# Bucketed attention and a rational FFN on one core: the maxima of every pair one slot sooner, their transposition behind the values' first group

## The chip, the cores and the metric

One core of one Trainium2 chip runs the whole program in one launch. The metric is the device time of one execution in microseconds (us), as the median of several runs. The host only rearranges the inputs (q and k transposed per pair of heads, v by blocks of 128 rows) and puts a few small constants together.

## The reference, cut to what matters

```python
q_bits = (einsum('bhsd,dk->bhsk', q, proj) > 0)        # 6 bits a row
k_bits = (einsum('bhsd,dk->bhsk', k, proj) > 0)
mask   = bucket(q_bits)[..., :, None] == bucket(k_bits)[..., None, :]
scores = where(mask, (q @ k.T) / sqrt(64), -1e9)
scores = scores - scores.max(-1)
attn   = exp(scores);  attn = attn / (attn.sum(-1) + 1e-9)
x      = (attn @ v) as (tokens, heads * 64)            # 3072 x 512
h      = x @ w_in                                      # 3072 x 2048
g      = (a0 + a1 h + a2 h^2 + a3 h^3) / (1 + |b0||h| + |b1| h^2 + 1e-6)
out    = g @ w_out
```

There are 4 batches of 8 heads, 768 rows each, head dimension 64.

## The kernel before, in words

The 32 heads are worked in 16 *pairs* (p = 0 to 15), two heads at a time on the 128 partitions. q and k are split into a high part in a short float format and a low part (`high` on ScalarE, `low` on VectorE), and both parts are moved by DMAs into the operands Q1, K1 (high) and Q2, K2 (high and low crossed), so that two products together give exact scores.

The mask is folded into the product. `bits` multiplies q and k of two pairs with the projection (TensorE tile psb) and VectorE compares with zero (tile mb); this is done once for two pairs, in frames of even p. `penalties` scales one half of mb by 2 to the 60th on ScalarE, and `maskrows` moves the rows into rows 64 to 75 of Q1 and 64 to 76 of K1, with four DMAs. A product over 76 rows then has a huge negative term wherever a bit differs.

The row maximum has to be known before the scores are exponentiated. `maxstep` computes, for one of the twelve (head, block of 128 query rows), the 768 products of the high parts (two matmuls, tile psm) and VectorE reduces them to one column of M[p] (tile m). When the twelve columns are there, `shift_turn` transposes M[p] on TensorE (one matmul with the identity, tile pst, in PSUM tag "s"; for pair 15 in tag "psa"), VectorE copies it with the sign turned (tile mt), and `shift_rows` moves it by a DMA into row 76 of Q1. From then on the scores come out with the maximum already taken off.

`scores` does one of twelve steps (half of the query rows, block of 128 keys): for either head two matmuls (tile pss, tag "s", three PSUM buffers) and one exponential on ScalarE (tile E, f32). GpSimd adds the E of neighbouring steps (tile acc). `values` multiplies E with v (tile psv): six steps' values stand together as one group of 24 matmuls, once behind step 5 and once behind step 11. `values_out` copies the result (col, xo), `sums` adds up acc with a column of ones (psu), and DMAs store x and the sums to DRAM. Meanwhile `weights` loads blocks of w_in and w_out (64-bit floats), turns them into f32 and splits each into a high and a low part, on ScalarE and VectorE (tiles wr, ws, wi_hi, wi_lo, wo_d). After pair 15 the FFN runs (`Ffn.rest`, tiles psh and pso); nothing in it is touched.

The order of all this is written out by hand. `plan` (lines 474 to 481) is a list of places: `at(p, s, f, ...)` puts the call f at place 12 p + s, and the calls are issued in the order of their places. I call the places 12 f to 12 f + 11 *frame* f: in it the scores of pair f stand at whole places 0 to 11. Every engine, and SyncE with its DMA queue, works in this order. The places are in the tables `MID` (lines 41 to 48, the pairs in the middle), `FIRST` and `LAST` (the exceptions). Preparation runs ahead: for pair p the high and low parts, bits, penalties, mask rows and the first maxima stand in frame p - 2, the rest of the maxima, the transposition and its DMA in frame p - 1.

Two kinds of buffers matter for the order. PSUM tag "psa" has two buffers; each maxstep takes one, and so does psb. So a maxstep's product waits until the reduction two maxsteps before has ended. PSUM tag "s" has three buffers; each head of a scores step takes one, and so do psu and pst. So a head's products wait until the tile three takes before has been read.

The lines that are touched are 42 to 46 (the places of maxima, low, penalties, maskrows, shift_turn and of four steps of weights), 59 (two places for pairs 2 and 3) and 491 and 516 (which place a maxstep and a transposition take).

Of the kernel before, what the change touches and what calls it, by code (L numbers as in the profile page):

```python
# [38 lines left out]
ACCS = 5  # L39

MID = dict(
    group=6, values=[0.66, 0.05], values_out=3.5, maxima=7.17,
    maxima_steps=[0, 1.15, 1.73, 2.64, 3.32, 5.08, 5.86, 6.98, 8.0, 8.84, 10.26, 11.37], sums=14.65, sums_store=17.37,
    high=[-0.41, 1.19], low=[1.06, 3.35], bits=2.81, penalties=4.05, high_move=1.9, maskrows=5.61, second_low=-2.2,
    second_high=2.69, load_v=10.99, shift_turn=8.61, shift_rows=8.82, load=9.0, recips=[20.0, 22.0, 23.0],
    weights=[[1.44, 4.0, 4.1, 5.09, 5.49, 7.11, 9.5, 9.75, 17.5], [8.05, 10, 10.65, 11.5, 12.38, 14.29, 16.34, 19.32, 21.22]],
    weights_last=[0.5, 0.8, 1.0, 1.2],
)

# [2 lines left out]
    high_move=4.53, maskrows=8.2, second_low=4.25, second_high=4.35, load_v=4.78, group=2,  # L52
    values=[2.35, 2.65, 2.32, 2.35, 0.35, 0.61], values_out=3.02, high1=[-0.27, -5.58], low1=[11.24, 4.95],
    high_move1=20.05, load2=21.89, load3=3.8, penalties1=-6.57, maskrows1=3.69,
    weights=[[-5.7, 6.64, 6.7, 11.42, 12.19, 18.75, 21.75, 38.77, 44.13], [8.03, 9.04, 9.24, 11.12, 14.81, 15.27, 15.99, 17.91, 46.81]],
    warm=6, warms=[3, 3, 3, 1, 1, 1], maxima00=[-4.26, -2.29, -4.17, 1.67, -1.15, 2.77], shift00=[2.15, 4.99],
    shift0=[3.67, 3.44], ahead=3, scores=[[3.68, 3.82, 7.26], [6.03, 8.25, 12.4]], pen01=[4.77, 14.55], comp01=3.35,
    second_high0=[-2.86, 2.12, -3.42, 3.45], load_v0=20.9, bits1=5.23, comp1=[15.82, 11.68],
    maxima0=[3.11, -1.97, -0.5, 2.14, 2.86, 3.25], turn1=[8.46, 13.26], rows1=[9.59, 14.35],
)  # L60

LAST = dict(
    group=6, values=[0.28, 0.44], values_out=1.39, vout14=3.03,
    tokens=[[-15.0, -11.5, -8.6, -7.4], [-7.43, -5.11, -2.83, -1.09], [1.1, 4.2, 5.45, 6.3]], terms=1.0, ffn=[13.61, 16.09, 16.14],
    sums=16.96, wide=8, share=11, third=0, sums14=14.69, weights14=1.44, sumst14=22.46,
# [38 lines left out]
def bucket_attention_then_rational_ffn(ctx, tc, qT, kT, v, proj, w_in, w_out, coef, consts, out):  # L104
# [56 lines left out]
    def operands_to_terms():  # L161
# [3 lines left out]

    tail.tile([P, 32], F32, tag="below", name="below")
    last = attention(tc, nc, raw, ps_b, tail, tokens, early, operands_to_terms, ffn, load, QF, KF, v, w_in, w_out, wo_d, ident, cst,
                     ones, prj, wi_hi, wi_lo, x_d, s_d, r_d, coefficients)
    ffn.rest(ctx, last)
# [3 lines left out]
def attention(ctx, tc, nc, raw, ps_b, tail, tokens, early, operands_to_terms, ffn, load, QF, KF, v, w_in, w_out, wo_d, ident, cst, ones, prj,  # L173
# [243 lines left out]
    def recips(bb):  # L417
        n = 2 * NHP * S // P
        s = tail.tile([P, n], F32, tag="rs", name=f"rs{bb}")
        nc.sync.dma_start(s, s_d[bb].rearrange("h (x c) -> (h x) c", c=n))  # L420
        yield
        z = tail.tile([P, n], F32, tag="rz", name=f"rz{bb}")
        nc.vector.tensor_scalar(out=z, in0=s, scalar1=0.0, scalar2=S * TINY, op0=ALU.is_equal, op1=ALU.mult)
        nc.vector.tensor_tensor(out=z, in0=s, in1=z, op=ALU.add)
        nc.vector.tensor_scalar(out=s, in0=s, scalar1=0.0, scalar2=1e-9, op0=ALU.is_gt, op1=ALU.mult)
        nc.vector.tensor_tensor(out=z, in0=z, in1=s, op=ALU.add)
        nc.vector.reciprocal(out=s, in_=z)
        yield
        nc.sync.dma_start(r_d[bb].rearrange("h (x c) -> (h x) c", c=n), s)
        yield  # L430
# [45 lines left out]
    def at(p, s, f, *args):  # L476
        plan.setdefault(12 * p + s, []).append((f, args))

    def spread(p, steps, gen):
        for s in steps:  # L480
            at(p, s, lambda g: next(g, None), gen)

    for p in range(NPAIR):
        mid = 0 < p < NPAIR - 1
        n = MID["group"] if mid else (FIRST if p == 0 else LAST)["group"]
        for s in range(12):
            if p > 0 or s >= FIRST["ahead"]:
                at(p, s, scores, p, s)

            if p > 1:  # L490
                at(p - 2, MID["maxima"] + MID["maxima_steps"][s] if p > 2 else FIRST["maxima2"] + FIRST["rate2"] * s, maxstep, p, s)
            if s % n == n - 1:
                for i in range(s - n + 1, s + 1):
                    at(p, s + (MID["values"][s // n] if mid else (FIRST if p == 0 else LAST)["values"][s // n]), values, p, i)
            if s % NT == NT - 1:
                at(p, s + (LAST["vout14"] if (p, s) == (NPAIR - 2, 11) else MID["values_out"] if mid else (FIRST if p == 0 else LAST)["values_out"]), values_out, p, s // NT)
        for hf in range(2):
            at(p, 6 * hf + 9, values_store, p, hf)
        if p < NPAIR - 1:
            at(p, MID["sums"] if p < NPAIR - 2 else LAST["sums14"], sums, p)  # L500
            at(p, MID["sums_store"] if p < NPAIR - 2 else LAST["sumst14"], sums_store, p)
        if p > 1:
            for t in range(2):
                at(p - 2, (MID if p > 2 else FIRST)["high"][t], high, p, t)
                at(p - 2, (MID if p > 2 else FIRST)["low"][t], low, p, t, nc.vector if p > 2 else nc.gpsimd)
            if p % 2 == 0:
                at(p - 2, (MID if p > 2 else FIRST)["bits"], bits, p)
                at(p - 2, (MID if p > 2 else FIRST)["penalties"], penalties, p)
            at(p - 2, (MID if p > 2 else FIRST)["high_move"], high_move, p)
            at(p - 2, (MID if p > 2 else FIRST)["maskrows"], maskrows, p)  # L510
        if p > 0:
            at(p - 1, (MID if p > 1 else FIRST)["second_low"], second_low, p)
            at(p - 1, (MID if p > 1 else FIRST)["second_high"], second_high, p)
            at(p - 1, (MID if p > 1 else FIRST)["load_v"], load_v, p)
        if p > 1:
            at(p - 1, MID["shift_turn"], shift_turn, p)
            at(p - 1, MID["shift_rows"], shift_rows, p)
        if p > 3:
            at(p - 4, MID["load"], load, p)
        if p % NHP == NHP - 1 and p + 1 < NPAIR:  # L520
            spread(p, MID["recips"], recips(p // NHP))
# [308 lines left out]
```

## Time and profile before

| | |
|---|---|
| median of 3 runs | 930.67 us (930.5 to 931.36) |
| the profiled execution | 929.79 us |
| its span, first to last instruction | 928.0 us |
| TensorE (PE) busy | 920.8 us, 99% |
| weight loads (PEld) | 699.9 us, 75% |
| VectorE (DVE) | 842.0 us, 91% |
| ScalarE (ACT) | 647.6 us, 70% |
| GpSimd (POOL) | 435.8 us, 47% |
| granted TensorE clock | 1.000 |

A line of the timeline gives the start and the length in us, the engine, the line of the kernel, the operation, the tiles written and read, the shapes, how many instructions are merged, and in brackets the engine's idle time before it with what ended that. Since every instruction is issued through a helper, all have the line L93; the tiles tell them apart. The length of a merged matmul row reaches to the modelled end of its last matmul, which overlaps with the next row's start: how long TensorE took is best read from one start to the next. PEld is the loading of weights, DVEq, SPq and the like are the engines' instruction queues. A line of `waits` says which engine and tile waited for which, for how many us in total, how often, and for how long at most.

### The profile page before, as it was taken

What the parts mean: (1) busy time and instruction counts of PE and PEld (TensorE: products, weight loads), DVE (VectorE), ACT (ScalarE), POOL (GpSimd) and SP (SyncE); (2) the same over time, 40 slices, a digit from 0 to 9 for tenths busy, and PEclk for the clock granted to TensorE, in tenths of its full rate; (3) what the DMA queues carried; (4) which work ended last, traced back from release to release, by engine and by line L of the source; (5) the groups of instructions that cost most, each with busy time, mean ns of one, the idle gap of its engine ahead of it and who ended that gap; (6) DMA issues with size and microseconds to landing.
All of it is one profiled execution on the core that took longest, in us unless ns stands there. A gap on an engine that the chain in (4) does not pass through costs nothing.

```text
span 928.0 us, 13694 instructions
## 1 busy us (share of the span) xinstructions
PE 920.8 (99%) x4678; PEld 699.9 (75%) x4678; DVE 842.0 (91%) x1029; ACT 647.6 (70%) x1229; POOL 435.8 (47%) x361
## 2 busy tenths in 40 slices
PE   8999999999999999999999999999999999999998
PEld 4666766666767676668888888888888888888886
DVE  6799889888988898888998999899999999998996
ACT  6567767676767766887767766776676677667664
POOL 5587878787788877622222232223222322232221
PEclk9999999999999999999999999999999999999999
DMA  6767878878877777545402100400040003001001
GB/s 197 214 181 219 229 230 230 223 214 212 242 212 225 229 195 233 163 155 197 163 1 81 56 1 1 136 2 0 1 137 1 1 34 102 1 1 46 1 1 46
DMA packets 51098, 111.57 MB, mean 120 GB/s; under 512 B 9330, under 2 KB 19942, under 8 KB 51028
## 3 DMA queue, kind: packets, MB, share of 16 engines
q1 hardware_dynamic: 50596, 110.34, 40.5%
q8 instruction: 37, 0.61, 0.3%
q10 hardware_dynamic: 432, 0.36, 0.1%
q14 instruction: 33, 0.27, 0.1%
HBM read 56.82 MB, written 21.17 MB: 84 GB/s over the span
## 4 chain that ended last, share of the span: by engine, by line
PE 93%; DVE 4%; DMA 1%; SPq 0%; ACT 0%; issue 0%; DVEq 0%; ACTq 0%
PE psh L93 28%; PE pso L93 28%; PE pss L93 14%; PE psv L93 12%; PE psm L93 7%; PE psu L93 2%; DVE m L93 2%; DMA wr<-w_in 1%; PE psb L93 1%; DVE ws L93 1%; DVE wr L93 0%; SPq L93 0%; PE psw L93 0%; PE pst L93 0%; ACT E L93 0%
## 5 line engine op out<-in xcount | busy, mean ns | idle before, releaser
L93 POOL TENSOR_TENSOR gl<-c,gh 128x512 fp32r<-128x512 f32 x95 | 133.2, 1402 | 387.0 <-ACT gh L93 371.0
L93 ACT ACTIVATE E<-pss 128x384 f32<-128x384 f32 x384 | 167.5, 493 | 105.8 <-PE pss L93 91.9
L93 PE MATMUL pso<-wo,gh 128*128 128x512 f32 x768 | 236.2, 390 | 0.0
L93 DVE TENSOR_REDUCE m<-psm 128x1 f32<-128x768 f32 x192 | 179.5, 948 | 31.4 <-PE psm L93 28.2
L93 POOL TENSOR_TENSOR acc<-E,E 128x384 f32<-128x384 f32 x124 | 155.6, 1273 | 85.9 <-ACT E L93 85.7
L93 PE MATMUL pss<-q,k 128*128 128x384 f32 (+2 forms) x768 | 171.3, 347 | 0.3 <-ACT E L93 0.3
L93 PEld LDWEIGHTS pso<-wo,gh 128*128 128x128 f32 x768 | 144.3, 188 | 29.9
L93 PEld LDWEIGHTS pss<-q,k 128*128 128x128 f32 (+2 forms) x768 | 134.6, 190 | 29.1 <-issue 17.0
L93 PE MATMUL psh<-xh,wi_hi 128*128 128x512 f32 x384 | 149.8, 390 | 0.0
L93 PE MATMUL psh<-xl,wi_hi 128*128 128x512 f32 x384 | 149.7, 390 | 0.0
L93 PE MATMUL psh<-xh,wi_lo 128*128 128x512 f32 x384 | 149.6, 390 | 0.0
L93 PE MATMUL pso<-wo,gl 128*128 128x512 f32 x384 | 149.1, 390 | 0.0
L93 ACT ACTIVATE h<-psh 128x512 f32<-128x512 f32 x96 | 57.4, 598 | 130.5 <-PE psh L93 130.3
L93 POOL TENSOR_TENSOR acc<-acc,E 128x384 f32<-128x384 f32 x123 | 136.6, 1129 | 5.9 <-ACT E L93 5.7
L93 DVE SCALAR_TENSOR_TENSOR c<-c,ab,r 128x512 f32<-128x512 f32 x96 | 135.6, 1413 | 0.0
L93 PE MATMUL psv<-E,v 128*64 128x385 f32 x768 | 131.9, 492 | 0.0
L93 PE MATMUL psm<-k,q 76*128 76x384 f32 (+1 forms) x384 | 102.4, 349 | 1.6 <-DVE m L93 1.0
L93 PEld LDWEIGHTS psv<-E,v 128*64 128x64 f32 x768 | 52.2, 137 | 65.3 <-issue 63.7
L93 DVE SCALAR_TENSOR_TENSOR w<-h,absb,w 128x512 f32<-128x512 f32 x96 | 74.0, 771 | 16.2 <-ACT w L93 15.9
L93 PEld LDWEIGHTS psh<-xh,wi_hi 128*128 128x128 f32 x384 | 72.1, 188 | 16.1 <-issue 1.2
L93 PEld LDWEIGHTS psh<-xh,wi_lo 128*128 128x128 f32 x384 | 72.2, 188 | 14.9
L93 PEld LDWEIGHTS psh<-xl,wi_hi 128*128 128x128 f32 x384 | 72.1, 188 | 14.9
(78 smaller groups left out, 1221.3 us busy)
## 6 DMA issues: line engine op xcount, KB each, us to landing
q<-q SPq DMA_DIRECT2D x45, 192.0 KB
k<-k SPq DMA_DIRECT2D x45, 192.0 KB
wr<-w_in SPq DMA_DIRECT2D x16, 512.0 KB
wr<-w_out SPq DMA_DIRECT2D x16, 512.0 KB
wo_d<-wr SPq DMA_DIRECT2D x16, 512.0 KB
wo<-wo_d SPq DMA_DIRECT2D x16, 512.0 KB
qkf<-qT SPq DMA_DIRECT2D x16, 384.0 KB
qkf<-kT SPq DMA_DIRECT2D x16, 384.0 KB
```

The costliest lines, as they stand in the source:

```text
L93: return self.tc.keep_in_program_order(issue(*args, **kwargs))
```

## The change

Only places change; no instruction is added or dropped.

- The twelve maxsteps of pair p (p from 3 on) had places 7.17, 8.32, 8.90, 9.81, 10.49, 12.25, 13.03, 14.15, 15.17, 16.01, 17.43 and 18.54 in frame p - 2 and on. Now the first one stands at 6.54, and each other one where the one before it stood. As 18.54 is 6.54 of the next frame, the twelve slots of a frame are the same as before, and each is used by the maxstep that had the next slot. Pair 3's first one stands at 6.9 of frame 1.
- shift_turn stands at 5.67 of frame p - 1 instead of 8.61, directly behind the first group of values (5.66). Pair 2 keeps 8.61. shift_rows keeps 8.82.
- For the first maxima the mask rows go out at 4.02 instead of 5.61. For this k's low part stands at 2.8 instead of 3.35, just ahead of bits (2.81), and the penalties at 3.05 instead of 4.05.
- Three VectorE steps of weights move behind the maxstep of place 5.43: two of a w_in block from 5.09 and 5.49 to 5.65 and 5.66, one of a w_out block from 16.34 to 17.645 (4.34 and 5.645 of the next frame).

```diff
 MID = dict(
-    group=6, values=[0.66, 0.05], values_out=3.5, maxima=7.17,
-    maxima_steps=[0, 1.15, 1.73, 2.64, 3.32, 5.08, 5.86, 6.98, 8.0, 8.84, 10.26, 11.37], sums=14.65, sums_store=17.37,
-    high=[-0.41, 1.19], low=[1.06, 3.35], bits=2.81, penalties=4.05, high_move=1.9, maskrows=5.61, second_low=-2.2,
-    second_high=2.69, load_v=10.99, shift_turn=8.61, shift_rows=8.82, load=9.0, recips=[20.0, 22.0, 23.0],
-    weights=[[1.44, 4.0, 4.1, 5.09, 5.49, 7.11, 9.5, 9.75, 17.5], [8.05, 10, 10.65, 11.5, 12.38, 14.29, 16.34, 19.32, 21.22]],
+    group=6, values=[0.66, 0.05], values_out=3.5,
+    maxima=[6.54, 7.17, 8.32, 8.9, 9.81, 10.49, 12.25, 13.03, 14.15, 15.17, 16.01, 17.43], sums=14.65, sums_store=17.37,
+    high=[-0.41, 1.19], low=[1.06, 2.8], bits=2.81, penalties=3.05, high_move=1.9, maskrows=4.02, second_low=-2.2,
+    second_high=2.69, load_v=10.99, shift_turn=5.67, shift_rows=8.82, load=9.0, recips=[20.0, 22.0, 23.0],
+    weights=[[1.44, 4.0, 4.1, 5.65, 5.66, 7.11, 9.5, 9.75, 17.5], [8.05, 10, 10.65, 11.5, 12.38, 14.29, 17.645, 19.32, 21.22]],
...
 FIRST = dict(
...
-    maxima0=[3.11, -1.97, -0.5, 2.14, 2.86, 3.25], turn1=[8.46, 13.26], rows1=[9.59, 14.35],
+    maxima0=[3.11, -1.97, -0.5, 2.14, 2.86, 3.25], turn1=[8.46, 13.26], rows1=[9.59, 14.35], turn2=8.61, third=6.9,
...
             if p > 1:
-                at(p - 2, MID["maxima"] + MID["maxima_steps"][s] if p > 2 else FIRST["maxima2"] + FIRST["rate2"] * s, maxstep, p, s)
+                at(p - 2, FIRST["maxima2"] + FIRST["rate2"] * s if p == 2 else FIRST["third"] if p == 3 and s == 0 else MID["maxima"][s], maxstep, p, s)
...
         if p > 1:
-            at(p - 1, MID["shift_turn"], shift_turn, p)
+            at(p - 1, MID["shift_turn"] if p > 2 else FIRST["turn2"], shift_turn, p)
             at(p - 1, MID["shift_rows"], shift_rows, p)
```

## The prediction, made before the result was known

> **What bounds the kernel now.** I read the page first, then the waits of the weight loads, then the timelines of one frame engine by engine (frame 8, an even one; a frame is the twelve plan places of one pair's scores), then the frames that differ from it: 1, 5, 7, 13, 14.
>
> ```profile
> PE 920.8 (99%) x4678; PEld 699.9 (75%) x4678; DVE 842.0 (91%) x1029; ACT 647.6 (70%) x1229; POOL 435.8 (47%) x361
> ...
> PEld psm L93 <- DVE m L93: 8.8, 28, 0.6
> ```
>
> TensorE carries the end: it is busy for 920.8 of 928.0 us. What it loses, it loses in rows that start later than they could. The second line names the one wait on VectorE that the change touches: the products for the maxima (psm) wait until an earlier maximum (m) gives its PSUM buffer back. So I cost every edit by one question: does it move a TensorE instruction? The maxima's twelve slots of a frame stay where they are (the new list is the old one shifted by an index), so of TensorE's work in the frames from 2 on the transposition alone moves; ScalarE, VectorE and SyncE get several moves.
>
> **The transposition leaves its old slot: 0.** Frame 8, TensorE, then the VectorE row that matters, then the transposed copy's group:
>
> ```profile
> 231.70 0.52 PE L93 MATMUL psm<-k,q 76*128 76x384 f32 x2
> ...
> 232.76 0.51 PE L93 MATMUL psm<-k,q 76*128 76x384 f32 x2
> 233.11 0.27 PE L93 MATMUL pst_None<-cst,m 128*12 128x128 f32 x1
> 233.26 0.61 PE L93 MATMUL psm<-k,q 76*128 76x384 f32 x2
> 233.71 0.52 PE L93 MATMUL pss<-q,k 77*128 77x384 f32 x2
> ...
> 232.25 0.96 DVE L93 TENSOR_REDUCE m<-psm 128x1 f32<-128x768 f32 x1
> ...
> L93 DVE TENSOR_SCALAR mt_None<-pst_None 12x128 fp32r<-12x128 f32 x13 | 3.5, 269 | 0.0
> ```
>
> From 233.11 to 233.71 pass 0.60 us for a transposition and a psm pair; the pair before takes 0.35 (232.76 to 233.11). So 0.25 looks free to win, in 12 frames 3.0 us. But the psm of 233.26 needs the buffer of 231.70, whose maximum ends at 232.25 + 0.96 = 233.21, and it starts 0.05 after that. And this maximum began 0.03 after its own product ended (231.70 + 0.52 = 232.22): VectorE was waiting for TensorE there, so getting VectorE ahead moves nothing. Without the transposition the pair still starts at 233.26 and still takes 0.61 instead of 0.51, the weight load that a wait exposes (frame 7's pair at 208.05, quoted below, waits with no transposition ahead and has 0.62). The transposition fills a hole. Bounds 0 and -3.0; I take 0, because the release can be read to 0.05.
>
> **The transposition behind the values: +0.3.** No row shows it there. The nearest are frame 8's scores behind the values; pair 15's transposition, which starts after a wait as it would after the values' end; and the start's one-row transpositions behind a values group:
>
> ```profile
> 229.81 0.97 PE L93 MATMUL pss<-q,k 77*128 77x384 f32 x4
> ...
> 374.20 0.28 PE L93 MATMUL pst<-cst,m 128*12 128x128 f32 x1 [0.32 <-DVE m L93]
> 374.23 0.96 PE L93 MATMUL pss<-q,k 77*128 77x384 f32 x4
> ...
> 25.18 1.47 PE L93 MATMUL pst<-cst,m 128*1 128x128 f32 x12
> 26.58 0.99 PE L93 MATMUL pss<-q,k 97*128 97x384 f32 x4
> ```
>
> Four score products end 0.97 after they start behind the values; with pair 15's transposition ahead they end 374.23 + 0.96 - 374.20 = 0.99 after the transposition's start. It hides under the first weight load and costs 0.02. The start's show the other end: twelve take until 26.58, 1.40 / 12 = 0.12 each, and the scores behind them are 0.99 long once more, so the exposed load is paid again: 0.2 in all at the most. Thirteen moved ones (pairs 3 to 15) give +0.3 or +2.6. I take +0.3, as the row of 374.20 has the same shape, 128*12. [...]
>
> **Penalties one place sooner, in even frames: +2.3.** They move from behind the exponentials of scores 4 (place 4.05) to behind those of scores 3 (3.05). ScalarE and TensorE of frame 8, then of frame 14, where another pass of similar length (xh) stands at that very place:
>
> ```profile
> 224.18 0.87 ACT L93 ACTIVATE E<-pss 128x384 f32<-128x384 f32 x2 [0.20 <-PE pss L93]
> 225.85 0.92 ACT L93 ACTIVATE mb<-mb,cst 128x768 fp32r<-128x768 f32 x1
> 226.68 0.67 ACT L93 ACTIVATE wr<-wr 128x512 int32<-128x512 uint32 x1
> ...
> 223.56 0.88 PE L93 MATMUL pss<-q,k 77*128 77x384 f32 x4
> 224.63 0.86 PE L93 MATMUL pss<-q,k 77*128 77x384 f32 x4
> ...
> 364.93 0.83 ACT L93 CAST xh<-y 128x768 fp32r<-128x768 f32 x1
> 365.66 0.88 ACT L93 ACTIVATE E<-pss 128x384 f32<-128x384 f32 x2
> ...
> 364.63 0.88 PE L93 MATMUL pss<-q,k 77*128 77x384 f32 x4
> 365.70 1.14 PE L93 MATMUL pss<-q,k 77*128 77x384 f32 x4
> ```
>
> The scores rotate through three PSUM buffers, so the second head of scores 5 needs the first exponential of scores 4. In frame 8 that one starts 224.18 - 223.56 = 0.62 after its products, undisturbed; in frame 14, behind xh, 365.66 - 364.63 = 1.03 after. There the row of scores 5 is 1.14 long instead of 0.86: 0.28 lost, on the path. xh holds ScalarE for 365.66 - 364.93 = 0.73, the penalties for 226.68 - 225.85 = 0.83, so 0.10 more: 0.38 a frame, in the frames of pairs 4, 6, ... 14: 6 x 0.38 = 2.3 (1.7 if the last 0.10 finds slack).
>
> **k's low part sooner (3.35 to 2.8).** VectorE in frames 8, 1, 5 and 13:
>
> ```profile
> 222.56 1.02 DVE L93 TENSOR_SCALAR mb<-psb,cst 128x768 fp32r<-128x768 f32 x1 [0.72 <-PE psb L93]
> ...
> 55.41 0.96 DVE L93 TENSOR_REDUCE m<-psm 128x1 f32<-128x768 f32 x1
> 56.28 0.95 DVE L93 TENSOR_TENSOR lo<-qkf,k 128x768 fp32r<-128x768 f32 x1
> 57.15 1.50 DVE L93 TENSOR_TENSOR wr<-ws,wr 128x512 fp32r<-128x512 f32 x1
> ...
> 63.21 0.94 DVE L93 TENSOR_REDUCE m<-psm 128x1 f32<-128x768 f32 x1
> ...
> 150.62 1.81 DVE L93 TENSOR_REDUCE m<-psm 128x1 f32<-128x768 f32 x2
> ...
> 341.09 1.81 DVE L93 TENSOR_REDUCE m<-psm 128x1 f32<-128x768 f32 x2
> ```
>
> It takes 57.15 - 56.28 = 0.87 of VectorE's time. In even frames it fills the 0.72 ahead of mb, which is put off by some 0.1 and is still there before the penalties: free. In frames 1, 5 and 13 VectorE has no gap there, the next maximum comes 0.87 later, and the product two slots on waits for it:
>
> ```profile
> 55.93 1.12 PE L93 MATMUL psm<-k,q 76*128 76x384 f32 x4
> ...
> 63.23 0.87 PE L93 MATMUL pss<-q,k 77*128 77x384 f32 x4
> 64.21 0.62 PE L93 MATMUL psm<-k,q 76*128 76x384 f32 x2
> ...
> 152.97 0.52 PE L93 MATMUL psm<-k,q 76*128 76x384 f32 x2
> ...
> 343.29 0.52 PE L93 MATMUL psm<-k,q 76*128 76x384 f32 x2
> ```
>
> Frame 13: the second of 341.09's maxima ends at 342.90. Add 0.87 and take off the 0.2 by which VectorE is ahead once the transposed copy (0.27, less the overlap of neighbours) has left the frame before: 343.57 against 343.29, 0.3 of wait and 0.1 of exposed load: +0.4. Frame 5 likewise: 152.43 becomes 153.10 against 152.97: +0.2. Frame 1: the second pair of 55.93 waits already for the maximum that ends at 56.37, so it takes the 0.87 in full. That delay eats the wait ahead of 64.21 (0.3, and 0.1 of load), but pair 3's extra maximum, put ahead of scores 7, then meets the same maximum (63.21 + 0.94 = 64.15): some 0.3 again. Frame 1: +0.8 (0.3 to 1.1). The extra pair's own 0.36 comes back in frame 14.
>
> **The rest: -0.3.** Frames 7, 8 and 14:
>
> ```profile
> 208.05 0.62 PE L93 MATMUL psm<-k,q 76*128 76x384 f32 x2
> 201.00 0.69 ACT L93 ACTIVATE ws<-wr 128x512 f32<-128x512 f32 x1 [0.79 <-DMA wr<-w_in]
> 234.48 0.78 SPq L93 DMA_DIRECT2D q<-mt_None  x1
> 371.86:379.88 8.02, 7.70 (x45) 5.22 (x44) 6.17 (x8) 7.81 (x18) 7.07 (x7) 1.00 0.60 200
> ```
>
> SyncE's queue no longer stands until 234.48 for the transposed copy, so the loads behind it go sooner, and frame 7's w_in, 0.79 late for ScalarE, may be in time; with it the wait at 208.05 goes. I take -0.3 (-0.5, two waits of 0.25, to +0.8 if w_in stays late, since scores 7 now need the buffer that the copy frees). The mask rows pass the sums' stores, which nobody waits for within the frame; the first maximum that needs them comes one slot sooner (232.76 - 231.70 = 1.06 us), they go 1.6 places sooner: free. The three weight steps on VectorE stay in the stretch of the values, behind a maximum instead of ahead of it: free. In frame 14 the 0.32 ahead of 374.20 goes, but ScalarE is busy for 7.81 of the 8.02 us behind it and sets when the next values can end: 0 (-0.5 at best).
>
> Sum: 0 + 0.3 + 2.3 + 0.4 + 0.2 + 0.8 - 0.3 = +3.7 on the profiled execution's 929.79, that is 933.5. The median of the runs is 930.67, 0.88 above, so I forecast 934.4. Its own range: with the low ends (1.7 for the penalties, 0.3 for frame 1, nothing for frames 5, 13 and the transposition, -0.5 twice) +1.0, 931.7; with the transposition at +2.6 instead of +0.3, +6.0, 936.7.
>
> **Rivals.** (1) No change: the penalties' delay doesn't reach TensorE, because the buffer comes free a tile sooner than I count. Without the 2.3 it is 932.1. For it: ScalarE waits 0.20 ahead of 224.18, so it isn't full there. Against: frame 14 shows the stall. (2) Faster: VectorE gets ahead wherever maxima are awaited, and these waits go: 3.0 at the old slot, 0.5 in frame 7, 0.4 in frame 1, 0.5 in frame 14, 0.2 where frame 5's maxima come late, 4.6 in all, with no charge for k's low part; 2.6 stay, so -2.0: 928.7. It decides from the point where the maximum of 232.25 could end 0.15 sooner. For it: the 0.72 filled. Against: that maximum follows its product by 0.03. (3) The transposition pays the values' exit again, 0.2 each: 936.7. For: the row of 26.58; against: that of 374.23. (4) The transposed copy, queued on VectorE behind three weight steps, holds scores 7 by its own 0.27 in 12 frames: +3.2, 937.6.
>
> **How the numbers follow.** Forecast 0.60, (1) 0.15, (2) 0.09, (3) 0.12, (4) 0.04. About 0.2% (1.9 us) is what a measurement here can tell from no change. Faster by more: (2), 0.09. Within it: (1) and the forecast's low end (0.08), 0.23. Slower: the rest, 0.68. The range 931.2 to 937.2 leaves out (2), (4) and a little at the edges.
>
> **What would show it.** In even frames the row of scores 5 is 1.2 us long; the psm pair of the old slot still starts 0.05 behind a maximum and is 0.61 long; behind the values the four scores end 0.99 after the transposition's start (near 1.2 if (3) holds); frame 1's second pair waits. It is wrong if scores 5 keep 0.86, or if the old slot's pair follows at 0.35.

## The result, and the profile after

The changed kernel takes 936.67 us (median of 6 runs, 935.67 to 937.14), the kernel before 930.75 in the same session (6 runs, 930.5 to 931.36): 1.0061 of the time before, 95% interval 1.0048 to 1.0074. It is slower, by 5.9 us; the forecast had 934.4 and +3.7. The profiled execution took 937.09, with a span of 935.3: 7.3 more than the profiled one of before.

First the page of the kernel after: engine, busy us and share of the span, number of instructions.

```profile
PE 923.6 (99%) x4678; PEld 697.7 (75%) x4678; DVE 844.3 (90%) x1029; ACT 646.4 (69%) x1229; POOL 438.8 (47%) x361
```

Little can be read from it: TensorE fills 99% of its span, as before, in a longer span. The waits of the kernel after say more (who waited for whom: us in total, times, the longest), and behind them the view of the transposed copy mt_None says who waited for that:

```profile
PEld psm L93 <- DVE m L93: 11.4, 28, 1.1
...
PEld pss L93 <- ACT E L93: 5.1, 13, 0.6
```
```profile
who waited for it (us, times):
  PEld pss L93: 2.1, 4
  PE pss L93: 0.7, 3
```

The products wait 2.6 us more for maxima (8.8 before), the scores wait for exponentials (5.1, 1.2 before), and in four places the scores wait for the transposed copy. To see where, I cut TensorE's rows into half frames: the first half of frame f runs from the start of the values' second group of frame f - 1 to that of the first group of frame f, the second half from there to the second group. The differences to before, in us, read from the starts of the values' rows (a half not named differs by less than 0.05):

| half frames | after minus before | what waits there |
|---|---|---|
| first halves of 2, 4, 6, 8, 10, 12 | 0.36, 0.40, 0.35, 0.36, 0.40, 0.35: 2.22 | scores 5, for the exponentials behind the penalties |
| first halves of 5, 9, 13 | 0.48, 0.64, 0.64 | a psm pair, for the maximum behind k's low part |
| first half of 1 | 1.77 | 0.8 the same; 1.0 a row that waits for a DMA |
| second half of 1 | 0.43 | pair 3's extra maximum, 0.36 |
| second halves of 3, 5, 9, 11 | 0.47, 0.82, 0.23, 0.45: 1.97 | scores 7, for the transposed copy (in 9 by 0.1, with 0.1 of exposed load) |
| second half of 7 | -0.03 | the copy's wait, in the place of one that before had |
| second half of 14, first of 15 | -0.58, +0.66 | the values end when ScalarE is done |
| FFN | 0.00 | |

The start up to the first values was 0.95 shorter in this execution, and the wait for the DMA, with 0.13 more in frame 0, gives that back; it came at another place or not at all in the runs below, so it belongs to the execution. The rest makes up the 7.3.

Frame 8, TensorE and ScalarE after. The row of 228.84 is scores 5; the two rows of 234.38 and 234.41 are the transposition and the scores behind the values; 237.30 holds the two psm pairs of the old slot:

```profile
227.77 0.88 PE L93 MATMUL pss<-q,k 77*128 77x384 f32 x4
...
228.84 1.23 PE L93 MATMUL pss<-q,k 77*128 77x384 f32 x4
...
234.38 0.28 PE L93 MATMUL pst_None<-cst,m 128*12 128x128 f32 x1
234.41 0.95 PE L93 MATMUL pss<-q,k 77*128 77x384 f32 x4
...
237.30 1.14 PE L93 MATMUL psm<-k,q 76*128 76x384 f32 x4
238.28 0.87 PE L93 MATMUL pss<-q,k 77*128 77x384 f32 x4
```
```profile
228.08 0.93 ACT L93 ACTIVATE mb<-mb,cst 128x768 fp32r<-128x768 f32 x1
228.91 0.87 ACT L93 ACTIVATE E<-pss 128x384 f32<-128x384 f32 x2
```

The penalties hold ScalarE from 228.08 to 228.91; the exponentials of scores 4 (227.77) start 1.14 after them, and scores 5 are 1.23 long. Behind the values the four scores end 234.41 + 0.95 - 234.38 = 0.98 after the transposition's start. The two psm pairs of the old slot still take 238.28 - 237.30 = 0.98, where two undisturbed ones would take 0.70. The second of them starts at 237.82, 0.06 behind the end of the maximum that frees its buffer: the hole is there, now empty.

Frame 13, TensorE and VectorE after: k's low part at 348.59, and the pair that waits for the maximum behind it.

```profile
348.13 0.87 PE L93 MATMUL pss<-q,k 77*128 77x384 f32 x4
348.84 0.52 PE L93 MATMUL psm<-k,q 76*128 76x384 f32 x2
349.20 0.86 PE L93 MATMUL pss<-q,k 77*128 77x384 f32 x4
350.45 0.62 PE L93 MATMUL psm<-k,q 76*128 76x384 f32 x2 [0.39 <-DVE m L93]
```
```profile
348.59 0.94 DVE L93 TENSOR_TENSOR lo<-qkf,k 128x768 fp32r<-128x768 f32 x1
349.45 1.81 DVE L93 TENSOR_REDUCE m<-psm 128x1 f32<-128x768 f32 x2
```

Frame 3, TensorE, VectorE and GpSimd after. The copy at 112.80 stands behind the last maximum (108.66) and three weight steps; the second scores behind the transposition wait for it:

```profile
111.63 0.28 PE L93 MATMUL pst_None<-cst,m 128*12 128x128 f32 x1
111.66 0.96 PE L93 MATMUL pss<-q,k 77*128 77x384 f32 x4
...
113.13 0.98 PE L93 MATMUL pss<-q,k 77*128 77x384 f32 x4 [0.16 <-DVE mt_None L93]
```
```profile
107.51 1.22 DVE L93 TENSOR_SCALAR wr<-wr 128x512 int32<-128x512 int32 x1
108.66 0.94 DVE L93 TENSOR_REDUCE m<-psm 128x1 f32<-128x768 f32 x1
109.52 0.67 DVE L93 TENSOR_TENSOR wr<-ws,wr 128x512 fp32r<-128x512 f32 x1
110.12 1.48 DVE L93 SCALAR_TENSOR_TENSOR ws<-ws,wr 128x512 int32<-128x512 int32 x1
111.74 1.13 DVE L93 CUSTOM_DVE_ANT_0 ws<-wr,ws 128x1024 uint16<-128x1024 uint16 x1
112.80 0.27 DVE L93 TENSOR_SCALAR mt_None<-pst_None 12x128 fp32r<-12x128 f32 x1
```
```profile
109.55 2.77 POOL L93 TENSOR_TENSOR acc<-acc,E 128x384 f32<-128x384 f32 x2
```

From 109.52 to 112.80 VectorE works nearly without a break, and the transposition's result, there at 111.63 + 0.28 = 111.91, lies for 0.9. In frame 8 the same copy is in time.

### The profile page after: what moved, and what is told of

It reads as the page before. It is cut to its first block, busy times and chain, and to the rows that moved or that the text cites. A ratio compares the mean times of both kernels' runs of the same rounds, so it can differ in the third digit from the quotient of the medians.

```text
span 935.3 us, 13704 instructions
## 1 busy us (share of the span) xinstructions
PE 923.6 (99%) x4678; PEld 697.7 (75%) x4678; DVE 844.3 (90%) x1029; ACT 646.4 (69%) x1229; POOL 438.8 (47%) x361
## 4 chain that ended last, share of the span: by engine, by line
PE 87%; DVE 7%; DMA 2%; issue 2%; ACT 2%; SPq 1%; DVEq 0%; ACTq 0%
PE psh L93 28%; PE pso L93 28%; PE pss L93 11%; PE psv L93 11%; PE psm L93 6%; DVE m L93 3%; PE psu L93 1%; PE psb L93 1%; ACT E L93 1%; DVE lo L93 1%; DVE ws L93 1%; DMA wr<-w_in 1%; SPq L93 1%; DVE wr L93 1%; DMA v<-v 0%
## 5 line engine op out<-in xcount | busy, mean ns | idle before, releaser
L93 POOL TENSOR_TENSOR gl<-c,gh 128x512 fp32r<-128x512 f32 x95 | 135.7, 1428 | 384.4 <-ACT gh L93 374.3
L93 POOL TENSOR_TENSOR acc<-E,E 128x384 f32<-128x384 f32 x124 | 144.9, 1187 | 91.9 <-ACT E L93 91.8
L93 POOL TENSOR_TENSOR acc<-acc,E 128x384 f32<-128x384 f32 x123 | 148.2, 1223 | 5.3 <-ACT E L93 5.2
L93 DVE SCALAR_TENSOR_TENSOR c<-c,ab,r 128x512 f32<-128x512 f32 x96 | 140.7, 1466 | 0.0
```

Source lines behind the costliest of these rows:

```text
L93: return self.tc.keep_in_program_order(issue(*args, **kwargs))
```

## The experiments

Theory A is the sum of the table above: penalties, k's low part, the copy behind the weight steps. The rivals stand in the expectations. Each run was timed beside the kernel before on the same chip; the ratio is against that, and so is "above before", which compares the two medians (the changed kernel is 5.9 above before). The kernel before had medians of 930.7 to 932.1 in these sessions, so times of different runs can't be compared without it. In every diff the lines with - are the changed kernel's unless said otherwise.

**The penalties put back** (mask rows just behind them):

```diff
-  penalties=3.05, maskrows=4.02
+  penalties=4.05, maskrows=4.06
```

> The changed kernel with the penalties back at 4.05 and the mask rows, which must follow them, at 4.06. Theory A (the penalties hold up scores 4's exponential and so scores 5): in each of the six even frames the 0.35 to 0.40 us that TensorE lost ahead of the first values go, the row of scores 5 is 0.86 again, and the median falls by 2.2 us, to about 934.4. Rival B (the loss of the even frames comes from k's low part or from mask rows that cross other transfers): the loss in these frames stays, and the median stays within 0.7 us of 936.67.

Measured: 935.05 us (10 runs, 933.69 to 941.05), 3.7 above before, which is 2.2 less than the changed kernel. The ratio, 1.0058 (1.004 to 1.0076), does not show this: it goes by all ten runs, and the four longest, 937.43 to 941.05, have a granted clock of 0.995 to 0.999. In the trace all six first halves are back at before's length, to 0.00 or 0.02, and the row of scores 5 in frame 8 is as before:

```profile
227.46 0.86 PE L93 MATMUL pss<-q,k 77*128 77x384 f32 x4
```

The other losses stay in sum, though not each: the second half of frame 5 is 0.23 longer than before (0.82 in the changed kernel), that of frame 9 0.66 (0.23). The trace settles what the ratio leaves open.

**The penalties alone, on the kernel before:**

```diff
-  penalties=4.05      (before)
+  penalties=3.05
```

> The kernel before with nothing but the penalties one place sooner (3.05 for 4.05); maxima, transposition, mask rows, k's low part and weights stay as before. Theory A (the penalties on ScalarE put off the exponentials of scores 4 and so the second head of scores 5, 0.35 to 0.40 in each of six even frames, whatever else changed): 2.2 more than before, and all of it in the first stages of frames 2, 4, 6, 8, 10 and 12. Rival B (the stall is only felt because the rest of the change has taken the slack of these frames): 0 to 0.6 more than before.

Measured: 933.13 (8 runs), ratio 1.0026 (1.0015 to 1.0036), 1.9 above before. The six first halves are 0.36, 0.40, 0.34, 0.36, 0.42 and 0.36 longer, 2.24 in all. Four other halves differ in the profiled run, to either side: the second ones of 7 (-0.45), 9 and 13 (+0.58 each) and 14 (+0.46). Frame 8, TensorE:

```profile
224.47 1.23 PE L93 MATMUL pss<-q,k 77*128 77x384 f32 x4
```

The same 1.23 with nothing else changed: the penalties' price is their own. Frame 7's old wait, which the forecast meant to win by an earlier w_in, is absent here too, although ScalarE waits longer for that w_in than before (1.71, 0.79 before). So the late w_in is not its cause. What differs is VectorE, whose three weight steps ahead of these maxima take 0.43, 0.68 and 0.68 here and 1.27, 1.49 and 1.35 before.

**k's low part put back:**

```diff
-  low=[1.06, 2.8]
+  low=[1.06, 3.35]
```

> The changed kernel with k's low part back at 3.35. Theory A (where VectorE has no idle time the low part pushes a maximum by 0.87 and the product two slots on waits): the losses ahead of the first values in frames 1 (0.8), 5 (0.5), 9 (0.64) and 13 (0.64) go, the even frames keep theirs, and the median falls by 2 to 2.6 us, to about 934.3. Rival B (VectorE comes late into these frames for other reasons): they stay, the median stays within 0.7 us of 936.67. If the low part, now behind mb, comes late for VectorE in even frames, the wait for the transposed copy appears there as well and takes back up to 2 us.

Measured: 935.73 (5 runs), ratio 1.0048 (1.0036 to 1.006), 4.4 above before. The waits of frames 1, 5, 9 and 13 are gone (0.00, -0.17, -0.02 and -0.01 against before). But the second halves of frames 1, 2 and 13 are 1.22, 1.22 and 0.83 longer than before. In frames 2 and 13 the copy is late; in frame 1, where the transposition keeps its old place, a psm pair waits 0.83 for a maximum. Frame 13 of this kernel, VectorE and TensorE:

```profile
347.96 1.83 DVE L93 TENSOR_TENSOR lo<-qkf,k 128x768 fp32r<-128x768 f32 x1
```
```profile
354.81 0.97 PE L93 MATMUL pss<-q,k 77*128 77x384 f32 x4 [0.55 <-DVE mt_None L93]
```

So VectorE has no room at either place: what k's low part doesn't take from the maxima ahead of the values it takes from the copy and the maxima behind them, and in this frame it is 1.83 long instead of 0.94.

**One weight step ahead of the last maximum:**

```diff
-  weights=[[..., 5.65, 5.66, 7.11, ...
+  weights=[[..., 5.42, 5.66, 7.11, ...
```

> The changed kernel with the shift-and-or step of a w_in block at 5.42 instead of 5.65, so that the maximum of place 5.43 and the low step of a w_out block stand between it and the addition that reads its result. Theory A (the addition directly behind its producer takes 1.14 us and waits 0.14 more, and this makes the copy of the transposition late, for whose buffer scores 7 wait): the addition takes 0.68 again, the waits of 0.3 to 0.5 behind the copy in frames 3, 5, 7 and 11 go, and the median falls by 1.2 to 2 us, to about 935.1. Rival B (the copy is late because the transposition itself, and GpSimd's sums beside it, come where they do): the waits stay, within 0.6 us of 936.67.

Measured: 938.02 (5 runs), ratio 1.0072 (1.006 to 1.0084), 6.7 above before. The copy's waits in frames 3, 7 and 11 stay (0.44 and 0.47 longer halves in 3 and 11); 5 drops to 0.24; frame 14's second half goes from -0.58 to +0.34. What I expected of the copy here didn't come. Frame 3 of this kernel, VectorE and GpSimd:

```profile
112.37 1.35 DVE L93 CUSTOM_DVE_ANT_0 ws<-wr,ws 128x1024 uint16<-128x1024 uint16 x1
```
```profile
110.39 2.77 POOL L93 TENSOR_TENSOR acc<-acc,E 128x384 f32<-128x384 f32 x2
```

The adding step does not fall to the 0.68 that theory A gave it, although the maximum and another step now stand between it and its producer: it takes 1.35. So its length does not come from standing directly behind its producer. What it does come from is in the last section.

**All three weight steps back where before had them** (the change moves three steps of weights, not four as the list of touched lines says):

```diff
-  weights=[[..., 5.65, 5.66, ...], [..., 17.645, ...]]
+  weights=[[..., 5.09, 5.49, ...], [..., 16.34, ...]]
```

> The changed kernel with only the three weight steps of VectorE back at 5.09, 5.49 and 16.34 (4.34 of the next frame); k's low part and the penalties stay sooner. Theory A (the transposed copy is late because it is queued behind these steps): the waits of scores 7 for the copy in frames 3, 5, 7 and 11 go, 0.45 + 0.8 + 0.2 + 0.45 = 1.9 less than the changed kernel, some 934.8; the waits for k's low part and the penalties stay as they are. Rival B (the copy is late because VectorE has fallen behind by k's low part): the stages of frames 3 and 11 stay 0.45 longer than before, and with the steps ahead of the maximum again frames 5, 9 and 13 lose more: 936.7 or above.

Measured: 940.57 (4 runs), ratio 1.0093 (1.0079 to 1.0108), 8.5 above before, where theory A had some 934.8. And with these steps, k's low part and the penalties all put back, so that only the maxima and the transposition are changed:

```diff
-  low=[1.06, 2.8], penalties=3.05, maskrows=4.02, weights as above
+  low=[1.06, 3.35], penalties=4.05, maskrows=4.06, weights as above
```

> The changed kernel with k's low part back at 3.35, the penalties at 4.05 (mask rows at 4.06) and the three weight steps back at 5.09, 5.49 and 16.34; what stays of the change is that the maxima stand one slot sooner and that the transposition stands behind the values' first group. Theory A (the loss is made of penalties, k's low part and the copy that is late behind the weight steps, and the transposition costs nothing behind the values nor brings anything at its old slot): the only stage of TensorE that stays longer than before is frame 1's second one, by pair 3's extra maximum, some 0.4; the time is 930.5 to 931.7 where before has 930.7 to 931.3. The stages of frames 3, 5, 11 with the late copy go back by 0.45, 0.8 and 0.45. Rival B (the new order of maxima and transposition itself is the loss, as scores 7 need the buffer that the copy frees): 0.2 to 0.5 a frame stay, 933 to 935.

Measured: 946.22 (4 runs), ratio 1.0153 (1.0135 to 1.0172), 14.1 above before. My expectation failed by 15 us. Of the 15.0 that the profiled run is longer than before, 4.1 are in the second half of frame 14, where a wait was followed by half the clock (last section). The waits of the two kernels, first the three steps alone put back, then all of it:

```profile
PE pst_None L93 <- DVE m L93: 3.1, 6, 0.8
```
```profile
PE pst_None L93 <- DVE m L93: 9.6, 12, 1.6
```

Frame 8 of the latter, VectorE and TensorE:

```profile
233.29 1.48 DVE L93 SCALAR_TENSOR_TENSOR ws<-ws,wr 128x512 int32<-128x512 int32 x1
234.70 0.94 DVE L93 TENSOR_REDUCE m<-psm 128x1 f32<-128x768 f32 x1
```
```profile
235.70 0.28 PE L93 MATMUL pst_None<-cst,m 128*12 128x128 f32 x1 [0.65 <-DVE m L93]
```

With the weight steps ahead, the last maximum ends after the values, and the transposition stands at the head of TensorE's queue and waits. So moving these steps isn't an extra of the change but its condition: directly behind the values the transposition needs VectorE to be done with the maxima first. The steps then stand ahead of the copy.

**Only the adding step behind the copy:**

```diff
-  weights=[[..., 5.65, 5.66, 7.11, ...
+  weights=[[..., 5.65, 5.68, 7.11, ...
```

> The changed kernel with nothing but the weights' adding step at 5.68, behind the transposed copy. Theory A (the copy is late behind the weight steps): the stages of frames 3, 5, 9 and 11 lose 0.45, 0.6 to 0.8, 0.2 and 0.45 of their length, some 1.9 in all, against the changed kernel; 934.8 where that has 936.7; penalties and k's low part cost what they did. Rival B (the copy's lateness comes from something that stands before the last maximum, as k's low part): these stages stay, 936.2 to 937.2.

Measured: 934.47 (6 runs, 934.28 to 935.0), ratio 1.0039 (1.0027 to 1.0051), 3.75 above before, 2.2 less than the changed kernel. Frame 3, VectorE and TensorE:

```profile
110.74 0.28 DVE L93 TENSOR_SCALAR mt_None<-pst_None 12x128 fp32r<-12x128 f32 x1 [0.34 <-PE pst_None L93]
110.95 0.72 DVE L93 CUSTOM_DVE_ANT_0 ws<-wr,ws 128x1024 uint16<-128x1024 uint16 x1
```
```profile
111.61 0.86 PE L93 MATMUL pss<-q,k 77*128 77x384 f32 x4
```

The copy now waits for the transposition and not the other way round; the scores of 111.61 follow without a wait. The second halves of frames 3, 5, 9 and 11 are back within 0.03 of before, frame 7's is 0.46 shorter than before. The copy's lateness was the queue ahead of it, as theory A has it. This is the steadiest of the kernels, and the change with its one clear mistake mended.

**The same, with penalties and k's low part put back:**

```diff
-  low=[1.06, 2.8], penalties=3.05, maskrows=4.02   (weights 5.65, 5.68)
+  low=[1.06, 3.35], penalties=4.05, maskrows=4.06  (weights 5.65, 5.68)
```

> The changed kernel with k's low part back at 3.35, the penalties at 4.05 (mask rows at 4.06), and the weights' adding step on VectorE (1.13 us where it follows its producer directly) at 5.68, behind the transposed copy of 5.67 and no longer ahead of it. The two runs before showed that the weight steps can't go back ahead of the last maximum, since the transposition behind the values then waits for it 0.7 us a frame. Theory A (the copy is late by what is queued ahead of it on VectorE, and 1.1 us less of that is enough): the waits of scores 7 for the copy are gone, in frames 3 and 11 (0.45 each) and those that k's low part at 3.35 brought in frames 1, 2 and 13 (1.2, 1.2, 0.8); what stays is the extra pair of frame 1 (0.4) and some small change in frames 14 and 15: 930.5 to 932. Rival B (VectorE is short of time between the values and scores 8, and the adding step now holds the first maximum instead): the waits go to the psm products of the same stages, 934 or above.

Measured: 934.30 (12 runs; 930.26 to 938.14, and one of 2922.35 that nothing here explains and that the ratio leaves out), ratio 1.0036 (1.002 to 1.0051), 3.6 above before. The copy's waits are gone, but in frames 1 and 5 products for maxima wait instead (second halves +1.21 and +1.12), much as rival B says. In frame 5 one of these waits is not for VectorE, and what it is for is open. The lowest runs, 930.26 and 930.70, are about where theory A puts it; the median isn't, and the profiled run shows one reason. TensorE and VectorE of frame 9, then windows from 248 on (us of the stretch, busy time of each engine, then the granted clock):

```profile
249.66 0.91 PE L93 MATMUL psm<-k,q 76*128 76x384 f32 x2 [1.43 <-DVE m L93]
```
```profile
247.26 1.48 DVE L93 TENSOR_TENSOR lo<-qkf,q 128x768 fp32r<-128x768 f32 x1 [1.12 <-DMA q<-lo]
```
```profile
248.00:250.00 2.00, 0.57 (x3) 0.34 (x2) 2.00 (x3) 0.85 (x2) 1.46 (x2) 0.95 1.09 219
250.00:252.00 2.00, 2.00 (x8) 1.98 (x7) 2.00 (x3) 0.00 (x0) 0.58 (x1) 0.50 0.76 159
...
256.00:258.00 2.00, 2.00 (x12) 0.80 (x10) 1.69 (x2) 0.00 (x0) 1.14 (x1) 0.85 0.21 45
```

A DMA that VectorE waited for came 1.1 late, TensorE stood for 1.43, and the granted clock went to 0.50 until some 256.6. Frame 9's halves are 2.86 and 2.29 longer than before. Without these 5.1 the run's 935.75 would be 930.6: as before, no gain.

**The transposition at its old place, all else moved:**

```diff
-  shift_turn=5.67
+  shift_turn=8.61
```

> The changed kernel with the transpositions back at 8.61 and all else moved. Theory A (the transposition is free in both places, what its move costs is the copy's wait alone): the waits behind the copy go, frames 3, 5 and 11 lose nothing ahead of their second values, the maxima's pair behind the transposition still starts 0.05 behind a maximum, and the median falls by 1.2 to 2 us, to about 935.1. Rival B (the transposition behind the values saves the exposed load at its old slot): the median rises, by up to 3 us, to 939.5.

Measured: 939.88 (5 runs), ratio 1.01 (1.0085 to 1.0115), 8.5 above before, 2.6 more than the changed kernel and not the 1.2 to 2 less of theory A. Nearly every second half is 0.2 longer than before. Frame 8:

```profile
238.86 0.27 PE L93 MATMUL pst_None<-cst,m 128*12 128x128 f32 x1
...
239.47 0.86 PE L93 MATMUL pss<-q,k 77*128 77x384 f32 x4
...
240.62 0.97 PE L93 MATMUL pss<-q,k 77*128 77x384 f32 x4
```

The transposition lies in its hole as before (239.47 - 238.86 = 0.61); what is new is the 240.62, scores 10 of pair 8, which wait. The two heads of scores 10 wait for other engines than before. The list has pair 7; in both traces the weight loads of pairs 7 and 8 wait alike:

```
before  pss7_10_0 [waits DVE]         pss7_10_1 [waits Activation]
here    pss7_10_0 [waits Activation]  pss7_10_1 [waits DVE]
```

The first head now gets the buffer of scores 9's first head and the second the transposition's. Why the three buffers are dealt out otherwise here I didn't settle. Frame 7 lost 1.4 more in this run, which I did not follow up.

**The hole itself.** Three kernels tried to win the 0.25 of the old slot. In two the psm pairs are spread over scores 9 to 11: before (transposition at its old place) and the kernel with only maxima and transposition changed. In the third the slot of 7.17 stands ahead of scores 7, in the kernel with the adding step behind the copy and with penalties and k's low part put back.

```diff
-  maxima 7.17, 8.32, 8.9, 9.81, 10.49, 12.25
+  maxima 7.17, 8.32, 9.2, 10.2, 11.03, 12.25     (spread, twice)
+  maxima 6.9,  8.32, 8.9, 9.81, 10.49, 12.25     (sooner)
```

> The kernel before with nothing but the maxima of 8.9, 9.81 and 10.49 moved to 9.2, 10.2 and 11.03; its transposition stays at 8.61, now with scores behind it. Theory A (the transposition and the wait lie in the same hole of 0.25, so either alone brings nothing): the transposition's 0.25 takes the place of the hole, 930.2 to 931.6, as before. Rival B (the exposed weight load of the pair goes as well, or the transposition hides under the scores' weight load): 0.1 to 0.25 a frame less, 927.8 to 929.6.

> The kernel of the run before this one, with the maxima's places 8.9, 9.81 and 10.49 at 9.2, 10.2 and 11.03, so that the pair of products which waits for the maximum of two slots before (0.35 us from row to row, released 0.05 behind the maximum's end, 0.1 longer for the exposed weight load) has scores ahead of it. Theory A (the hole that the transposition filled is 0.15 of wait and 0.1 of exposed load in each of 12 frames, and VectorE has the time): the frames' second stages are 0.25 shorter, 3.0 in all, 927.7 to 928.9. Rival B (VectorE or ScalarE is what sets the pace of that stretch, so the wait only moves to the values or to another pair): within 0.6 of the run before, or above it.

> The kernel of the run before this one with the maximum of 7.17 at 6.9, so that the product at 8.9, which waits for it, finds its buffer free; the two products of 6.54 and 6.9 then stand together, where the buffers are free since the values. Theory A (the old slot's hole of 0.15 wait and 0.1 exposed weight load goes, and VectorE has caught up by then): 0.25 less in 12 frames' second stages, 3.0 less than the run before, 927.5 to 929. Rival B (VectorE, having the copy, the adding step and two maxima close together, is as late for 8.9 as before, and for 8.32 too): the same time as the run before or up to 2 more.

Measured, in this order: 937.74 (5 runs), ratio 1.0061 (1.0047 to 1.0074); 944.67 (6 runs), 1.0145 (1.0121 to 1.0169), near the 1.0153 of its parent; 939.16 (6 runs, 933.9 to 949.76, the longest at a granted clock of 0.987), 1.0074 (1.0046 to 1.0101). None won anything. First frame 8 of before with the maxima spread:

```profile
239.19 0.27 PE L93 MATMUL pst_None<-cst,m 128*12 128x128 f32 x1
239.50 1.03 PE L93 MATMUL pss<-q,k 77*128 77x384 f32 x4
...
240.93 0.98 PE L93 MATMUL pss<-q,k 77*128 77x384 f32 x4
```

The hole is gone, but ahead of scores the transposition costs 0.31 and an exposed load (these scores are 1.03 long, the ones before it 0.87), and the next scores wait for the buffer it took: second halves 0.5 longer. Then frame 8 with the slot of 7.17 sooner:

```profile
234.66 0.86 PE L93 MATMUL psm<-k,q 76*128 76x384 f32 x4
235.37 0.86 PE L93 MATMUL pss<-q,k 77*128 77x384 f32 x4
236.22 0.62 PE L93 MATMUL psm<-k,q 76*128 76x384 f32 x2
```

The two pairs of 234.66 now follow each other without a wait (0.71 for both), and the hole stands at the next pair, 236.22. There are three psm pairs with one scores step between them and two buffers, and in either order one of the three waits for a maximum of 0.95. Most second halves are 0.2 longer than the parent's.

## Why the prediction was right, and where it was not

The verdict, slower, and its largest term were right for the reason given; the sum was 2.2 too low by the medians and 3.6 by the profiled executions, in terms that can be named. The 936.67 lie at the upper end of the forecast's own range, 931.7 to 936.7, and that is luck: this end is the forecast with the transposition at +2.6, which cost 0.2 at most. What filled the place is the copy (+2.0), the rest of k's low part (+1.15) and pair 3's extra maximum (+0.4), and the range had none of them.

| term | forecast | measured in the trace | shown by |
|---|---|---|---|
| transposition leaves the old slot | 0 | 0 | the hole, still there in frame 8 |
| transposition behind the values | +0.3 | +0.2 at most | 0.98 from its start to the scores' end |
| penalties | +2.3 | +2.2 | taken back: 0 to 0.02 a frame; alone on before: 2.24 |
| k's low part | +1.4 | +2.55 | taken back: the four waits go |
| pair 3's extra maximum | 0 | +0.4 | second half of frame 1, in all kernels that keep k's low part at 2.8 |
| weight steps on VectorE | 0 | +2.0 | only the adding step put behind the copy: the waits go |
| SyncE, w_in, frame 7 | -0.3 | 0 | the penalties alone, on before, lose the same wait |

- *The transposition.* Both steps held: 0.98 from its start to the scores' end in frame 8 (0.98 to 1.01 in all thirteen), where 0.99 was forecast and 0.97 is what the scores take alone. Rival (3), the exit paid twice at 0.2 each, is out.
- *The penalties.* Right in mechanism, place and size.
- *k's low part.* Right in mechanism, too small in size. The step that failed is "take off the 0.2 by which VectorE is ahead", which the copy's leaving was to bring: frame 13's pair waits from 349.91 (349.20 plus the 0.71 that the scores before took, 348.84 - 348.13) to 350.45, which is 0.54 and not 0.3. Such a lead does not show. And frame 9, odd like 5 and 13, was not looked at: 0.64.
- *The weight steps.* "The three weight steps on VectorE stay in the stretch of the values, behind a maximum instead of ahead of it: free" is the step that failed most. They are free for the maxima and not for the copy, which stands behind them. Rival (4) named the mechanism, at a chance of 0.04, with 0.27 a frame in all twelve; it came in four frames (3, 5, 7, 11) with 0.45 to 0.8 each and in frame 9 with 0.2, and not at all in the others. In frame 7 it took the place of the wait that the forecast counted as won.
- *Frame 7.* The forecast laid its wait at 208.05 to the late w_in. With the penalties alone moved w_in is later still and the wait is gone, so that step was wrong too.
- *"The extra pair's own 0.36 comes back in frame 14"* contradicts the sentence on frame 14, that ScalarE sets when the next values can end. The latter held. Frame 14 after, TensorE: the values' 24 products, 4.10 long elsewhere, take 4.76 because they start sooner and end with ScalarE.

```profile
383.37 4.76 PE L93 MATMUL psv<-E,v 128*64 128x385 f32 x24
```

The trace's terms make 7.3, the medians 5.9. The gap is that the profiled run of before was 0.96 below its median and that of the changed kernel 0.42 above its own. For the latter frame 5's copy may be the cause (0.82 in the profiled run, 0.2 in the three others with the same weight steps); what made the former short is open.

## What to carry to other kernels

When a step is moved to stand directly behind another, price its consumer's queue and not only its own: here the matmul was free, and the copy that ends its buffer's use stood behind three steps of another job. A gap that something fills is only won if nothing else needs it: ask which wait made the gap, and whether it stays when the filling goes. Where a schedule has frames of several kinds, work out every one: k's low part in frame 9 and the copy in frames 3, 5 and 11 make up most of what was missed.

## What the runs showed of the hardware

- *One wait can cost its multiple.* The 1.43 us of TensorE's idle time in frame 9 above were followed by a granted clock of 0.50 for some 6.8 us, and the two halves of the frame grew by 5.1. A wait of 2.01 in the kernel with only maxima and transposition changed was likewise followed by 0.50 for some 6.8; waits of 1.61 in that same kernel, of 1.50 (three weight steps put back) and of 1.99 (before with the maxima spread) were followed by 1.00. So the length of the single wait does not tell whether 0.50 follows: it did behind 1.43 and not behind 1.99. What decides it is not shown. Of the twelve runs of the kernel with the 1.43, the two of 930.26 and 930.7 have a mean granted clock of 1.000, the two of 937.4 and 938.14 one of 0.995 and 0.996. That the spread of some medians comes from this is likely and not shown for each run.
- *VectorE beside GpSimd.* The weights' adding step takes 1.13 in frame 3, where GpSimd adds until 109.55 + 2.77 = 112.32, 0.72 behind the copy in the mended kernel, and 0.68 at 230.42 in frame 8 of before, where GpSimd's additions had ended at 227.85 + 2.50 = 230.35. The step wr<-wr took 1.22 in frame 3 of the kernel after, against 0.43 in its frame 8, and k's low part 1.83 in the frame 13 that had it back, where two of GpSimd's additions run from 347.96 to 350.65, against 0.94. So the length of these steps depends on what GpSimd does meanwhile, and a group's mean (0.75 for the adding step before), from which I priced, hides it. The adding step of frame 3 also shows by how much. It lasted 1.13 when 0.58 of the addition were left at its start (111.74 to 112.32), 1.35 when 0.79 were left (112.37 to 113.16, one step ahead of the last maximum) and 0.72 when 0.17 were left (110.95 to 111.12, behind the copy): each time 0.55 more than what was left. For wr<-wr it is 0.30 both times: 1.22 with 0.92 left (107.51 to 107.43 + 1.00 = 108.43), 0.43 with 0.13 left (230.36 to 229.47 + 1.02 = 230.49). By an estimate from the 0.68, at half its rate while the addition lasts, the adding step would have taken some 0.97 and 1.07 in the first two; the 1.13 and 1.35 are more than that. Why a running addition holds these steps up is not shown.
